# Four passes instead of six for the batch tails' second token product, a last MLP that ends block by block, and idle matmuls in other forms

## The chip, the cores and the metric

The kernel runs on one core of a Trainium2 chip, as one program. The metric is the device time of an execution in microseconds (us); runs of the same kernel are compared by their median. The engines are TensorE (PE in the rows; PEld is its weight load), VectorE (DVE), ScalarE (ACT), GpSimd (POOL) and SyncE (SP), which before the change issues every transfer of the kernel.

## The reference

Eight batches of 576 tokens go through sparse attention with 8 heads of 64 (heads 0 to 3 see the last 32 positions, heads 4 to 7 see positions of the same residue modulo 32), and then through a mixer in float32:

```
xt = x.transpose(0, 2, 1)
h = np.maximum(xt @ w_tok1, 0.0) @ w_tok2
u = x + h.transpose(0, 2, 1)
h2 = np.maximum(u @ w_ch1, 0.0) @ w_ch2
return (u + h2).astype(np.float32)
```

Here x is 576 tokens by 512 channels for each batch; w_tok1 is 576 x 256, w_tok2 256 x 576, w_ch1 512 x 1536 and w_ch2 1536 x 512.

## The kernel before

**Precision.** A float32 operand is kept as two fp32r tiles, a high part and the rest (`hh` and `hl`, `t2h` and `t2l`, `gh` and `gl`, `w2h` and `w2l`). A product is then three passes on TensorE: high by high, high by rest, rest by high. Weights arrive as 64-bit numbers; `convert` and `load_split` turn a piece of 128 x 512 into the two tiles with two steps on ScalarE, two on VectorE, one cast on ScalarE and one subtraction on GpSimd.

**Stages.** Tokens of a batch are cut into a main group of 512 (`MAIN`) and a tail of 64 (`TAIL`). The first token product (`tok1`, L489) and the second one for the main group (`tok2`, L515 and L520) work on one batch at a time, as does the channel MLP (`mlp`): twelve `up_proj` (L688: 12 matmuls into one bank, then `gh` on ScalarE at L691 and `gl` on VectorE at L692) and twelve `down_proj` (L703: 3 matmuls into each of the four accumulators `acc0` to `acc3`, one for each block of 128 channels). `down_proj(fc)` stands two steps behind `up_proj(fc)`. After the last `down_proj` VectorE adds the residual to each accumulator (L720) and SyncE writes the block out (L725, L729).

**Tails.** The 64 tail tokens of a batch are handled by `tok2_tail` (L524), which stands behind the first `up_proj` of the batch's MLP (behind the second `down_proj` step in batch 0). It makes 6 matmuls of 128x512 into one bank (L530); VectorE adds x in place (L532) and SyncE stores the 64 rows to a DRAM tile `u` (L533). In the eighth MLP `load_tails` (L538) reads the eight pieces back, `tail_u` (L543) transposes them, and a ninth MLP treats all 8 x 64 tail tokens as one group of 512. Its outputs are written by `out_tail` (L729), in rows of 64 tokens.

**Order.** TensorE, VectorE, ScalarE and GpSimd run in the order in which the code is written; the dictionary `after` puts pieces of other work behind given steps of an MLP. SyncE's order is chosen by a scheduler after the first stage. The strided heads of batches 2 to 7 are computed on GpSimd (products, L375) and VectorE (sums, L423 and L447) beside the MLPs.

**The start.** Before the first token product TensorE waits for x. `keep_busy(17)` (L640) fills that time with 17 matmuls on a zero bf16 tile `still` (L603). `still`, `idle_t` and these matmuls carry no result.

Of the kernel before, what the change touches and what calls it, by code (L numbers as in the profile page):

```python
# [10 lines left out]
F32 = mybir.dt.float32  # L11
F32R = mybir.dt.float32r
U32 = mybir.dt.uint32
# [3 lines left out]
ALU = mybir.AluOpType  # L17
# [3 lines left out]
B, H, S, D = 8, 8, 576, 64  # L21
HL = 4
ST = 32
DM = H * D
DT = 256
DF = 1536
P = 128
# [11 lines left out]
NCC = DM // P  # L39
NFC = DF // P  # L40
DV = D + 1
NSC = 5
# [9 lines left out]
MAIN = 512  # L52
TAIL = S - MAIN
# [3 lines left out]
def attn_mixer_kernel(ctx, tc, qkT, vw, qs, ks, vs, qksT, vsP, mask, mask2, w1, w2, wt1, wt2, outT):  # L57
    nc = tc.nc

    const = ctx.enter_context(tc.tile_pool(name="const", bufs=1))  # L60
# [17 lines left out]
    t1h = const.tile([P, NSC, DT], F32R, name="t1h")  # L78
    t1l = const.tile([P, NSC, DT], F32R, name="t1l")

    t2h = const.tile([P, 2, S + TAIL], F32R, name="t2h")
    t2l = const.tile([P, 2, S + TAIL], F32R, name="t2l")


    ud = [dram.tile([TAIL, DM], F32, name=f"u{b}") for b in range(B)]

    xd = [dram.tile([2 * S, DM], F32, name=f"x{p}") for p in range(B // 2)]

# [66 lines left out]

    def t2_tail(raws):

        src = (wt2[P * c:P * c + P, MAIN:].bitcast(U32).unsqueeze(1).to_broadcast([P, 2, 2 * TAIL]) for c in range(2))
        return load_split(raws, lambda: (t2h[:, :, MAIN:], t2l[:, :, MAIN:]), 4 * TAIL, *src)

    def w1_piece(raws, q, c):

# [361 lines left out]
    def tok2_tail(ps_t, x_t, h, b):  # L524

        pu = ps_t.tile([P, 512], F32, name="t")
        for m in range(2):
            hh, hl = h[m]
            for k, (l, r) in enumerate(((t2h, hh), (t2l, hh), (t2h, hl))):
                nc.tensor.matmul(pu, l[:, m, MAIN:], r, start=(m == 0 and k == 0), stop=(m == 1 and k == 2))  # L530
        rs = slice(64 * (b % 2), 64 * (b % 2) + 64)
        nc.vector.tensor_tensor(out=x_t[rs, NSC - 1], in0=pu[rs], in1=x_t[rs, NSC - 1], op=ALU.add)  # L532
        nc.sync.dma_start(out=ud[b], in_=x_t[rs, NSC - 1])  # L533

    def load_tails(u_t):

        for b in range(B):
            nc.sync.dma_start(out=u_t[64 * (b % 2):64 * (b % 2) + 64, b // 2], in_=ud[b])  # L538

    def tail_u(pool, ps_t, u_t, cc):  # L540
        pu = ps_t.tile([P, 512], F32, name="t")
# [40 lines left out]
    with tc.tile_pool(name="first", bufs=4) as first, \  # L582
         tc.tile_pool(name="raws", bufs=4, side="right") as raws, \
         tc.tile_pool(name="ps_a", bufs=6, space=PSUM) as ps_a, \
         tc.tile_pool(name="ps_m", bufs=2, space=PSUM) as ps_m:
        still = first.tile([P, 512], BF16, name="still", bufs=1)
        nc.vector.memset(still, 0.0)
        mask2_sb = first.tile([RP, RP], F32, name="mask2_sb", bufs=1)
        masks = first.tile([P, 5 * 64], BF16, name="masks", bufs=1)
        nc.sync.dma_start(out=mask2_sb, in_=mask2)  # L590
        loaded = [strided_load(first, 0, hp) for hp in range(2)]
        nc.sync.dma_start(out=mask_sb, in_=mask)
        nc.gpsimd.tensor_copy(
            out=mask2_b.rearrange("p (c k) -> p c k", k=RP), in_=mask2_sb.unsqueeze(1).to_broadcast([RP, 3, RP]))
        for c in range(5):
            nc.gpsimd.tensor_copy(out=masks[:, 64 * c:64 * c + 64], in_=mask_sb[:, FIRST.get(c, 0)])


        idle_t = ps_m.tile([P, 512], F32, name="t")

        def keep_busy(n):
            for _ in range(n):
                nc.tensor.matmul(idle_t, still[:, :P], still, start=True, stop=True)  # L603

        keep_busy(WARM)

# [12 lines left out]
        def steps(*gens):  # L619
            for g in gens:  # L620
                next(g, None)


        also = {0: [early[0], *units[:2], early[1], *units[2:], early[2], early[3]],
                4: [early[0]], 5: [early[0], early[4]], 6: [early[1]], 7: [early[1]], 8: [early[5]], 9: [early[2]], 10: [early[3], early[2]],
                11: [early[3]], 12: [early[4]], 13: [early[5], early[4]], 15: [early[5]]}
        for i in range(len(work) + 4):
            for k in (0, 2, 4):
                if 0 <= i - k < len(work):
                    if k == 2 and i >= BUSY:  # L630
                        keep_busy(2)
                    next(work[i - k], None)
            if i == 11:
                load_x(x_t, 0, slice(HL * D, DM))
                steps(early[6])
            steps(*also.get(i, ()))
        u = []
        mixes = [tok2(up0, ps_a, x_t, h, cc, u) for cc in range(NCC)]
        steps(early[7], mix)
        keep_busy(17)  # L640
        steps(mix, early[6], early[8], mix, early[6], mix, *mixes, mix, early[7], mix, *pieces[:4], early[7])
        steps(mixes[0], mixes[1], early[8], mixes[2], pieces[0], mixes[3], early[8])

# [18 lines left out]

    ps_t = Banks()

    def mlp(us, after, write):


        acc = [ps_acc.tile([P, MAIN], F32, name=f"acc{cc}") for cc in range(NCC)]
        g, res, count = {}, [], [0]

        def done():
            for f in after.get(count[0], ()):
                f()
            count[0] += 1

        def middle():
            for f in after.get(count[0] - 0.5, ()):
                f()

        def up_proj(fc, bank="h"):  # L680
            fs = slice(P * fc, P * fc + P)
            ph = ps_t.tile([P, MAIN], F32, name=bank)
            for cc in range(NCC):
                if cc == 2:
                    middle()
                uh, ul = us[cc]
                for k, (l, r) in enumerate(((w1h, uh), (w1l, uh), (w1h, ul))):
                    nc.tensor.matmul(ph, l[:, cc, fs], r, start=(cc == 0 and k == 0), stop=(cc == NCC - 1 and k == 2))  # L688
            gh = up.tile([P, MAIN], F32R, name="gh")
            gl = up.tile([P, MAIN], F32R, name="gl")  # L690
            nc.scalar.activation(out=gh, in_=ph, func=AF.Relu)  # L691
            nc.vector.scalar_tensor_tensor(out=gl, in0=ph, scalar=0.0, in1=gh.bitcast(F32), op0=ALU.max, op1=ALU.subtract)  # L692
            g[fc] = (gh, gl)
            done()

        def down_proj(fc):
            gh, gl = g.pop(fc)
            for cc in range(NCC):
                if cc == 2:
                    middle()  # L700
                cs = slice(P * cc, P * cc + P)
                for k, (l, r) in enumerate(((w2hl["h"], gh), (w2hl["h"], gl), (w2hl["l"], gh))):
                    nc.tensor.matmul(acc[cc], l[:, fc, cs], r, start=(fc == 0 and k == 0), stop=(fc == NFC - 1 and k == 2))  # L703
            if 4 <= fc < 4 + NCC:
                uh, ul = us[fc - 4]
                o_t = up.tile([P, MAIN], F32, name="ot", bufs=NCC)
                on_gpsimd(ALU.add, out=o_t, in0=uh.bitcast(F32), in1=ul.bitcast(F32))
                res.append(o_t)
            if fc < NFC - 1:
                done()  # L710

        up_proj(0)
        up_proj(1, "t")
        for fc in range(NFC):
            if fc + 2 < NFC:
                up_proj(fc + 2)
            down_proj(fc)

        for cc, o_t in enumerate(res):
            nc.vector.tensor_tensor(out=o_t, in0=acc[cc], in1=o_t, op=ALU.add)  # L720
            write(cc, o_t)
        done()

    def out_main(b):
        return lambda cc, o_t: nc.sync.dma_start(out=outT[P * cc:P * cc + P, S * b:S * b + MAIN], in_=o_t)  # L725

    def out_tail(cc, o_t):
        to = outT[P * cc:P * cc + P].rearrange("p (b s) -> p b s", s=S)
        nc.sync.dma_start(out=to[:, :, MAIN:], in_=o_t.rearrange("p (b t) -> p b t", t=TAIL))  # L729

    def strided_lane(pool, b, gs, got):
        for hp in range(HL // 2):
# [60 lines left out]
    for b in range(B):  # L793
# [52 lines left out]
        for i in range(24):  # L846
            if b or i >= 16:
                at(i, some_strided, 20 if b < 2 else 23)
        mlp(u, after, out_main(b))
        x_t, h, u = x_next["x"], x_next["h"], x_next["u"]  # L850
    mlp(u, {}, out_tail)


_OUT = (DM, B * S)
# [71 lines left out]
```

## Time and profile before

| what | value |
|---|---|
| median of 3 runs | 823.19 us (821.32 to 823.48) |
| profiled execution, first to last instruction | 821.2 us |
| TensorE busy | 799.8 us (97%) |
| VectorE, GpSimd, ScalarE busy | 449.8, 404.6, 229.6 us |
| mean granted TensorE clock | 0.996 |
| transfers | 80.80 MB, 98 GB/s on average |

The profile gives the span of the profiled execution, and no separate time for it; the three timed runs lie 0.1 to 2.3 us above that span. Matmuls overlap in the records: one of 128x512 is shown as 390 ns long, while the next one starts some 227 ns after it. So the distance between starts, not the duration, is the price of a matmul in a stream.

### The profile page before, as it was taken

The page shows a single profiled execution, that of the slowest core. Times are in us where ns is not written, and L with a number is a line of the kernel's source. Part 1 is how long each engine was busy: PE and PEld are TensorE (multiplying, and loading weights), DVE is VectorE, ACT ScalarE, POOL GpSimd, SP SyncE. Part 2 cuts the span into 40 slices and gives each one's busy share as a digit, 9 for nine tenths or more (in the row PEclk, how much of TensorE's full clock was granted, in tenths as well). Part 3 has the DMA queues.
Part 4 walks back from the last instruction along what each step waited for, and adds up shares of the span by engine and source line. Part 5 has one row for each costly group of instructions (what it writes and reads, how often), then busy time and mean ns, then how long its engine had stood idle before and what let it go on. Part 6 is the DMA issues. An engine that isn't in the chain of part 4 may idle for free.

```text
span 821.2 us, 14373 instructions
## 1 busy us (share of the span) xinstructions
PE 799.8 (97%) x5839; PEld 648.0 (79%) x5839; DVE 449.8 (55%) x990; ACT 229.6 (28%) x483; POOL 404.6 (49%) x305
## 2 busy tenths in 40 slices
PE   9899998999999999999999999999999999999996
PEld 6577776878788888887888888888888888888885
DVE  6866745777687576655856566667561213113112
ACT  5667755232121222212213021222121211102100
POOL 2223345959778694768767866686730102002000
PEclk9999999999999999999999999999999999999999
DMA  9586545233601440245113500551032003001002
GB/s 302 169 278 197 184 130 203 82 129 104 206 30 59 134 117 30 98 129 180 34 52 107 152 29 31 164 159 60 1 94 76 1 1 109 1 0 52 1 0 52
DMA packets 59166, 80.80 MB, mean 98 GB/s; under 512 B 22244, under 2 KB 37348, under 8 KB 59100
## 3 DMA queue, kind: packets, MB, share of 16 engines
q1 hardware_dynamic: 59100, 79.89, 31.0%
q8 instruction: 46, 0.75, 0.4%
q14 instruction: 20, 0.16, 0.1%
HBM read 60.41 MB, written 19.33 MB: 97 GB/s over the span
## 4 chain that ended last, share of the span: by engine, by line
PE 83%; DVE 4%; DMA 3%; ACT 3%; issue 1%; POOL 1%; SPq 1%; POOLq 0%; ACTq 0%; DVEq 0%
PE acc L703 33%; PE h L688 30%; PE t L520 5%; PE t L489 5%; PE t L688 3%; PE t L515 1%; PE t L530 1%; PE t L299 1%; DMA w_raw<-in_w 1%; PE t L271 1%; PE t L289 1%; DVE xhl L477 1%; ACT gh L691 1%; ACT w_rest L118 1%; DMA sa<-in_ks 1%
## 5 line engine op out<-in xcount | busy, mean ns | idle before, releaser
L375 POOL TENSOR_TENSOR sprod<-sa,ss 128x576 f32<-128x576 f32 (+8 forms) x108 | 153.2, 1450 | 78.2 <-issue 40.0
L375 POOL TENSOR_TENSOR sprod<-sa 128x576 f32<-128x576 f32 (+8 forms) x108 | 159.6, 1508 | 40.1 <-DVE ss L423 11.1
L692 DVE SCALAR_TENSOR_TENSOR gl<-h,gh 128x512 fp32r<-128x512 f32 x99 | 68.3, 690 | 200.6 <-ACT gh L691 200.6
L703 PE MATMUL acc<-gh,w2h 128*128 128x512 f32 x432 | 170.8, 395 | 0.0
L703 PE MATMUL acc<-gh,w2l 128*128 128x512 f32 x432 | 168.5, 390 | 0.0
L703 PE MATMUL acc<-gl,w2h 128*128 128x512 f32 x432 | 168.5, 390 | 0.0
L688 PE MATMUL h<-uh,w1h 128*128 128x512 f32 x396 | 158.0, 399 | 2.3 <-DVE gl L692 2.3
L688 PE MATMUL h<-ul,w1h 128*128 128x512 f32 x396 | 155.0, 391 | 0.0
L688 PE MATMUL h<-uh,w1l 128*128 128x512 f32 x396 | 154.6, 390 | 0.0
L691 ACT ACTIVATE gh<-h 128x512 fp32r<-128x512 f32 x99 | 59.0, 596 | 308.6 <-PE h L688 308.6
L375 POOL TENSOR_TENSOR ot<-uh,ul 128x512 f32<-128x512 f32 x36 | 49.7, 1388 | 139.7 <-DMA out_t<-ot 91.7
L703 PEld LDWEIGHTS acc<-gh,w2l 128*128 128x128 f32 x432 | 81.2, 188 | 17.3
L703 PEld LDWEIGHTS acc<-gh,w2h 128*128 128x128 f32 x432 | 81.3, 188 | 17.1
L703 PEld LDWEIGHTS acc<-gl,w2h 128*128 128x128 f32 x432 | 81.3, 188 | 16.3
L688 PEld LDWEIGHTS h<-uh,w1h 128*128 128x128 f32 x396 | 74.5, 188 | 19.4 <-DVE gl L692 3.1
L423 DVE TENSOR_REDUCE ss<-sprod 128x9 f32<-128x576 f32 (+8 forms) x108 | 80.1, 779 | 15.5 <-POOL sprod L375 15.2
L688 PEld LDWEIGHTS h<-ul,w1h 128*128 128x128 f32 x396 | 74.5, 188 | 16.1
L688 PEld LDWEIGHTS h<-uh,w1l 128*128 128x128 f32 x396 | 74.5, 188 | 14.6
L447 DVE TENSOR_REDUCE sa<-sprod 128x64 f32<-128x576 f32 (+8 forms) x108 | 79.5, 778 | 7.9 <-POOL sprod L375 7.7
L507 DVE TENSOR_TENSOR ul<-t,uh 128x512 fp32r<-128x512 f32 x36 | 24.8, 690 | 48.8 <-ACT uh L506 48.7
L489 PE MATMUL t<-xhl,t1h 128*128 128x512 f32 x144 | 45.2, 398 | 5.1 <-DVE xhl L474 2.4
L477 DVE TENSOR_TENSOR xhl<-x,xhl 128x512 fp32r<-128x512 f32 x32 | 37.5, 1191 | 12.9 <-ACT xhl L471 12.7
(122 smaller groups left out, 879.4 us busy)
## 6 DMA issues: line engine op xcount, KB each, us to landing
out_t<-ot SPq DMA_DIRECT2D x36, 256.0 KB
w_raw<-in_w SPq DMA_DIRECT2D x17, 512.0 KB
lqk<-in_qkT SPq DMA_DIRECT2D x20, 416.0 KB
lv<-in_vw SPq DMA_DIRECT2D x20, 390.0 KB
x<-x SPq DMA_DIRECT2D x28, 256.0 KB
xhl<-in_w SPq DMA_DIRECT2D x7, 512.0 KB
sa<-in_qs SPq DMA_DIRECT2D x6, 576.0 KB
sa<-in_ks SPq DMA_DIRECT2D x6, 576.0 KB
```

The costliest lines, as they stand in the source:

```text
L118: nc.scalar.activation(out=y_b[:, :, 0], in_=raw_b[:, :n, 3], func=AF.Identity, bias=below, scale=1.0 / 32)
L375: i = nc.gpsimd.tensor_tensor(op=op, **operands)
L423: nc.vector.tensor_reduce(out=s_t[:, i, :i + 1], in_=pr.rearrange("p (n d) -> p n d", d=D), axis=AX.X, op=ALU.add)
L447: nc.vector.tensor_reduce(out=o_t[:, i], in_=pr.rearrange("p (d n) -> p d n", n=i + 1), axis=AX.X, op=ALU.add)
L477: apart.append(nc.vector.tensor_tensor(out=xlo, in0=x, in1=xh.bitcast(F32), op=ALU.subtract))
L489: nc.tensor.matmul(ph[m], l[:, c, P * m:P * m + P], r, start=(c == 0 and k == 0), stop=(c == NSC - 1 and k == 1))
L507: nc.vector.tensor_tensor(out=ul, in0=pu, in1=uh.bitcast(F32), op=ALU.subtract)
L520: nc.tensor.matmul(pu, l[:, cs], r[:, m, :MAIN], start=False, stop=(m == 1 and k == 2), skip_group_check=True)
L688: nc.tensor.matmul(ph, l[:, cc, fs], r, start=(cc == 0 and k == 0), stop=(cc == NCC - 1 and k == 2))
L691: nc.scalar.activation(out=gh, in_=ph, func=AF.Relu)
L692: nc.vector.scalar_tensor_tensor(out=gl, in0=ph, scalar=0.0, in1=gh.bitcast(F32), op0=ALU.max, op1=ALU.subtract)
L703: nc.tensor.matmul(acc[cc], l[:, fc, cs], r, start=(fc == 0 and k == 0), stop=(fc == NFC - 1 and k == 2))
```

## The change

The edits, in the order of the diff:

- **Tail product.** `t2h` now holds, behind its 512 main columns, 64 columns of the high part and 64 of the rest of w_tok2's tail. One stationary operand of 128 columns therefore yields both products, in rows 0 to 63 and 64 to 127 of the bank. Two moving operands (`hh`, `hl`) and two chunks make 4 matmuls. VectorE adds x to the upper half; ScalarE copies the lower half to the other 64 rows of `x_t`; 128 rows are stored instead of 64. The piece `t2_tail` that is loaded and converted has 128 columns instead of 256.
- **Loading the tails.** 16 loads instead of 8, the second halves into two `xhl` tiles, and four additions of 128x512 on GpSimd.
- **Last MLP.** With `held=3` the last three `down_proj` are not done one after the other but block by block: nine matmuls for a channel block, then its addition and its write. The last block is added and written in two halves, the second of them issued by ScalarE.
- **Output layout.** The output keeps the main groups of all batches first and the tail group behind them, in rows of 512 tokens each; the host puts them in order.
- **Idle matmuls.** Instead of 17 on `still`: eight fp32r ones of 128x512 and four of 128x256 on parts of `t1h` and `t1l`, and then six on `still`.

```diff
-    t2h = const.tile([P, 2, S + TAIL], F32R, name="t2h")
-    t2l = const.tile([P, 2, S + TAIL], F32R, name="t2l")
+    t2h = const.tile([P, 2, MAIN + 2 * TAIL], F32R, name="t2h")
+    t2l = const.tile([P, 2, MAIN], F32R, name="t2l")
...
-    ud = [dram.tile([TAIL, DM], F32, name=f"u{b}") for b in range(B)]
+    ud = [dram.tile([2 * TAIL, DM], F32, name=f"u{b}") for b in range(B)]
...
-        src = (wt2[P * c:P * c + P, MAIN:].bitcast(U32).unsqueeze(1).to_broadcast([P, 2, 2 * TAIL]) for c in range(2))
-        return load_split(raws, lambda: (t2h[:, :, MAIN:], t2l[:, :, MAIN:]), 4 * TAIL, *src)
+        src = (wt2[P * c:P * c + P, MAIN:].bitcast(U32) for c in range(2))
+        return load_split(raws, lambda: (t2h[:, :, MAIN:MAIN + TAIL], t2h[:, :, MAIN + TAIL:]), 2 * TAIL, *src)
...
-            hh, hl = h[m]
-            for k, (l, r) in enumerate(((t2h, hh), (t2l, hh), (t2h, hl))):
-                nc.tensor.matmul(pu, l[:, m, MAIN:], r, start=(m == 0 and k == 0), stop=(m == 1 and k == 2))
-        rs = slice(64 * (b % 2), 64 * (b % 2) + 64)
-        nc.vector.tensor_tensor(out=x_t[rs, NSC - 1], in0=pu[rs], in1=x_t[rs, NSC - 1], op=ALU.add)
-        nc.sync.dma_start(out=ud[b], in_=x_t[rs, NSC - 1])
+            for k, r in enumerate(h[m]):
+                nc.tensor.matmul(pu, t2h[:, m, MAIN:], r, start=(m == 0 and k == 0), stop=(m == 1 and k == 1))
+        nc.vector.tensor_tensor(out=x_t[:TAIL, NSC - 1], in0=pu[:TAIL], in1=x_t[:TAIL, NSC - 1], op=ALU.add)
+        nc.scalar.copy(out=x_t[TAIL:, NSC - 1], in_=pu[TAIL:])
+        nc.sync.dma_start(out=ud[b], in_=x_t[:, NSC - 1])
...
-        for b in range(B):
-            nc.sync.dma_start(out=u_t[64 * (b % 2):64 * (b % 2) + 64, b // 2], in_=ud[b])
+        halves = [xp.tile([P, 2, DM], F32, name="xhl") for _ in range(2)]
+        for p in range(B // 2):
+            l_t = halves[p // 2][:, p % 2]
+            for b in (2 * p, 2 * p + 1):
+                rs = slice(TAIL * (b % 2), TAIL * (b % 2) + TAIL)
+                nc.sync.dma_start(out=u_t[rs, p], in_=ud[b][:TAIL])
+                nc.sync.dma_start(out=l_t[rs], in_=ud[b][TAIL:])
+            nc.gpsimd.tensor_tensor(out=u_t[:, p], in0=u_t[:, p], in1=l_t, op=ALU.add)
...
-        keep_busy(17)
+        rows = t1h[:, 0:2].rearrange("p c n -> p (c n)")
+        for n, (l, r, cols) in enumerate((
+                (t1h, rows, 0), (t1h, rows, 0), (t1h, rows, 0), (t1h, rows, 0), (t1l, rows, 1), (t1h, rows, 0), (t1l, rows, 1), (t1h, rows, 0),
+                (t1l, rows[:, :256], 0), (t1h, rows[:, :256], 1), (t1l, rows[:, :256], 0), (t1h, rows[:, :256], 1))):
+            nc.tensor.matmul(idle_t[:, :r.shape[1]], l[:, 2, P * cols:P * cols + P], r, start=True, stop=True)
+        for n in (0, 1, 2, 3, 0, 1):
+            nc.tensor.matmul(idle_t, still[:, P * n:P * n + P], still, start=True, stop=True)
...
+        def down_block(fc, cc):
+            gh, gl = g[fc]
+            cs = slice(P * cc, P * cc + P)
+            for k, (l, r) in enumerate(((w2hl["h"], gh), (w2hl["h"], gl), (w2hl["l"], gh))):
+                nc.tensor.matmul(acc[cc], l[:, fc, cs], r, start=(fc == 0 and k == 0), stop=(fc == NFC - 1 and k == 2))
...
-            down_proj(fc)
+            if fc < NFC - held:
+                down_proj(fc)
...
-            nc.vector.tensor_tensor(out=o_t, in0=acc[cc], in1=o_t, op=ALU.add)
-            write(cc, o_t)
+            for fc in range(NFC - held, NFC):
+                down_block(fc, cc)
+            parts = [slice(0, MAIN)] if not held or cc < NCC - 1 else [slice(0, MAIN // 2), slice(MAIN // 2, MAIN)]
+            for part in parts:
+                nc.vector.tensor_tensor(out=o_t[:, part], in0=acc[cc][:, part], in1=o_t[:, part], op=ALU.add)
+                write(cc, o_t, part)
...
+        def write(cc, o_t, part):
+            queue = nc.scalar if part.start else nc.sync
+            queue.dma_start(out=outT[P * cc:P * cc + P, MAIN * b + part.start:MAIN * b + part.stop], in_=o_t[:, part])
...
-    mlp(u, {}, out_tail)
+    mlp(u, {}, out_group(B), held=3)
```

The order of the instructions at three places follows; names are those of the code, with the number of the buffer behind them.

TensorE at the tail of batch 1, before: the last matmul of the first `up_proj`, the six of the tail, and the first of the second `up_proj`.

```order
L688 MATMUL h<-ul,w1h 128x512
L530 MATMUL t<-hh_1651,t2h 128x512
L530 MATMUL t<-hh_1651,t2l 128x512
L530 MATMUL t<-hl_1652,t2h 128x512
L530 MATMUL t<-hh_1653,t2h 128x512
L530 MATMUL t<-hh_1653,t2l 128x512
L530 MATMUL t<-hl_1654,t2h 128x512
L688 MATMUL t<-uh,w1h 128x512
```

The same place of the changed kernel:

```order
L699 MATMUL h<-ul,w1h 128x512
L529 MATMUL t<-hh_1651,t2h 128x512
L529 MATMUL t<-hl_1652,t2h 128x512
L529 MATMUL t<-hh_1653,t2h 128x512
L529 MATMUL t<-hl_1654,t2h 128x512
L699 MATMUL t<-uh,w1h 128x512
```

Two matmuls of 128x512 are gone, and nothing else stands differently there.

TensorE at its end, before: the last `down_proj`, whose four accumulators take turns.

```order
L703 MATMUL acc0_7424<-gh_7744,w2h_862 128x512
L703 MATMUL acc0_7424<-gl_7745,w2h_862 128x512
L703 MATMUL acc0_7424<-gh_7744,w2l_863 128x512
L703 MATMUL acc1_7425<-gh_7744,w2h_862 128x512
L703 MATMUL acc1_7425<-gl_7745,w2h_862 128x512
L703 MATMUL acc1_7425<-gh_7744,w2l_863 128x512
L703 MATMUL acc2_7426<-gh_7744,w2h_862 128x512
L703 MATMUL acc2_7426<-gl_7745,w2h_862 128x512
L703 MATMUL acc2_7426<-gh_7744,w2l_863 128x512
L703 MATMUL acc3_7427<-gh_7744,w2h_862 128x512
L703 MATMUL acc3_7427<-gl_7745,w2h_862 128x512
L703 MATMUL acc3_7427<-gh_7744,w2l_863 128x512
```

The end of the changed kernel: the last matmul of block 2 and the nine of block 3, whose `gh` and `gl` come from the last three `up_proj`.

```order
L711 MATMUL acc2_7433<-gh_7751,w2l_864 128x512
L711 MATMUL acc3_7434<-gh_7691,w2h_863 128x512
L711 MATMUL acc3_7434<-gl_7692,w2h_863 128x512
L711 MATMUL acc3_7434<-gh_7691,w2l_864 128x512
L711 MATMUL acc3_7434<-gh_7722,w2h_863 128x512
L711 MATMUL acc3_7434<-gl_7723,w2h_863 128x512
L711 MATMUL acc3_7434<-gh_7722,w2l_864 128x512
L711 MATMUL acc3_7434<-gh_7751,w2h_863 128x512
L711 MATMUL acc3_7434<-gl_7752,w2h_863 128x512
L711 MATMUL acc3_7434<-gh_7751,w2l_864 128x512
```

The 36 matmuls of the last three steps are the same in number. Each of the first three blocks is complete nine matmuls before the next one instead of three.

GpSimd at its end in the changed kernel; before, twelve additions at L375 stand there in a row.

```order
L375 TENSOR_TENSOR ot<-uh,ul 128x512 x4
L543 TENSOR_TENSOR x<-x,xhl 128x512 x4
L375 TENSOR_TENSOR ot<-uh,ul 128x512 x8
```

The four new additions stand ahead of the residual sums `ot` of the eighth and the ninth MLP.

## Rows read from the trace of the kernel before

**Rows 1.** The page: busy time by engine, and the chain by line.
```profile
PE 799.8 (97%) x5839; PEld 648.0 (79%) x5839; DVE 449.8 (55%) x990; ACT 229.6 (28%) x483; POOL 404.6 (49%) x305
...
PE acc L703 33%; PE h L688 30%; PE t L520 5%; PE t L489 5%; PE t L688 3%; PE t L515 1%; PE t L530 1%; PE t L299 1%; DMA w_raw<-in_w 1%; PE t L271 1%; PE t L289 1%; DVE xhl L477 1%; ACT gh L691 1%; ACT w_rest L118 1%; DMA sa<-in_ks 1%
```

**Rows 2.** TensorE's waits from 240 us to the end: total, times, longest (us).
```profile
PE h L688 <- DVE gl L692: 1.8, 1, 1.8
PE t L489 <- DVE xhl L477: 0.3, 1, 0.3
```

**Rows 3.** Timeline at the tail of batch 2: start and duration (us), instruction, idle before.
```profile
255.42 0.39 PE L530 MATMUL t<-hh,t2h 128*128 128x512 f32 x1
...
256.78 0.39 PE L688 MATMUL t<-uh,w1h 128*128 128x512 f32 x1
...
256.98 0.68 DVE L532 TENSOR_TENSOR x<-t,x 64x512 f32<-64x512 f32 x1
...
259.76 0.60 ACT L691 ACTIVATE gh<-t 128x512 fp32r<-128x512 f32 x1 [3.54 <-PE t L688]
```

**Rows 4.** The chain that ended last, at the tails of batches 0 and 1.
```profile
65.93 1.39 PE t L530 x6
...
165.79 1.36 PE t L530 x6
```

**Rows 5.** Timelines of ScalarE and VectorE behind the tail of batch 0.
```profile
67.03 0.87 ACT L118 ACTIVATE w_rest<-w_raw,small 128x512 uint8<-128x512 uint8 x1
...
67.77 0.67 DVE L532 TENSOR_TENSOR x<-t,x 64x512 f32<-64x512 f32 x1
...
73.60 0.52 ACT L342 ACTIVATE es<-es 126x378 f32<-126x378 f32 x1 [2.63 <-DVE es L341]
```

**Rows 6.** Timeline of GpSimd in the ninth MLP.
```profile
750.54 5.02 POOL L375 TENSOR_TENSOR ot<-uh,ul 128x512 f32<-128x512 f32 x4 [62.99 <-DMA out_t<-ot]
```

**Rows 7.** Timeline of the end.
```profile
807.36 0.69 DVE L692 SCALAR_TENSOR_TENSOR gl<-h,gh 128x512 fp32r<-128x512 f32 x1 [4.75 <-ACT gh L691]
...
812.91 2.73 DVE L720 TENSOR_TENSOR ot<-acc,ot 128x512 f32<-128x512 f32 x4 [4.85 <-PE acc L703]
...
813.63 3.35 SPq L729 DMA_DIRECT2D out_t<-ot  x4
...
814.47 0.39 PE L703 MATMUL acc<-gh,w2l 128*128 128x512 f32 x1
```

**Rows 8.** SyncE's waits from 680 us to the end.
```profile
SPq L921 <- DMA out_t<-ot: 3.2, 1, 3.2
```

**Rows 9.** Windows: busy us of each engine, granted clock, share and GB/s of transfers.
```profile
750.00:751.00 1.00, 1.00 (x6) 0.78 (x6) 0.81 (x2) 0.20 (x1) 0.46 (x1) 1.00 1.05 381
815.00:816.00 1.00, 0.00 (x0) 0.00 (x0) 0.64 (x1) 0.00 (x0) 0.00 (x0) 1.00 0.99 221
```

**Rows 10.** Timeline of SyncE: a tail of 64 rows stored, and the next issue.
```profile
685.84 0.47 SPq L533 DMA_DIRECT2D u<-x  x1
688.20 5.12 SPq L538 DMA_DIRECT2D x<-u  x8
```

**Rows 11.** A VectorE group that reads a bank, by form: busy us, mean ns.
```profile
L341 DVE TENSOR_TENSOR es<-t,em 126x252 f32<-126x252 f32 x8 | 3.4, 420 | 0.3
```

**Rows 12.** Timeline of the idle matmuls and what follows them.
```profile
34.17 3.61 PE L603 MATMUL t<-still 128*128 128x512 bf16 x16 [0.81 <-issue]
...
37.06 1.14 ACT L471 CAST xhl<-x 128x512 fp32r<-128x512 f32 x2
...
37.73 0.73 PE L489 MATMUL t<-xhl,t1h 128*128 128x512 f32 x2
```

**Rows 13.** Windows as in group 9, around TensorE's stretch at the lower clock.
```profile
104.77:108.18 3.41, 3.41 (x11) 2.66 (x10) 1.07 (x7) 2.28 (x7) 0.00 (x0) 0.50 0.34 112
...
108.20:818.10 709.90, 699.77 (x4821) 574.27 (x4819) 375.49 (x766) 158.81 (x341) 374.76 (x267) 1.00 0.26 80
38.00:60.00 22.00, 20.81 (x99) 15.67 (x99) 14.30 (x24) 13.67 (x26) 5.04 (x5) 1.00 0.78 258
```

More of the change, by code (lines that the diff above doesn't have):

```diff
@@ L663, in attn_mixer_kernel, with mlp @@
     ps_t = Banks()
-    def mlp(us, after, write):
+    def mlp(us, after, write, held=0):
         acc = [ps_acc.tile([P, MAIN], F32, name=f"acc{cc}") for cc in range(NCC)]
@@ L694, in up_proj @@
             done()
+        def down_block(fc, cc):
[3 more added lines that the diff above has]
+                nc.tensor.matmul(acc[cc], l[:, fc, cs], r, start=(fc == 0 and k == 0), stop=(fc == NFC - 1 and k == 2))
         def down_proj(fc):
-            gh, gl = g.pop(fc)
             for cc in range(NCC):
@@ L700, in down_proj @@
                     middle()
-                cs = slice(P * cc, P * cc + P)
-                for k, (l, r) in enumerate(((w2hl["h"], gh), (w2hl["h"], gl), (w2hl["l"], gh))):
-                    nc.tensor.matmul(acc[cc], l[:, fc, cs], r, start=(fc == 0 and k == 0), stop=(fc == NFC - 1 and k == 2))
+                down_block(fc, cc)
             if 4 <= fc < 4 + NCC:
@@ L716, in mlp, with out_group @@
                 up_proj(fc + 2)
-            down_proj(fc)
+            if fc < NFC - held:
+                down_proj(fc)
         for cc, o_t in enumerate(res):
-            nc.vector.tensor_tensor(out=o_t, in0=acc[cc], in1=o_t, op=ALU.add)
-            write(cc, o_t)
-        done()
[L724 to L729, printed above, removed]
+            for fc in range(NFC - held, NFC):
+                down_block(fc, cc)
+            parts = [slice(0, MAIN)] if not held or cc < NCC - 1 else [slice(0, MAIN // 2), slice(MAIN // 2, MAIN)]
+            for part in parts:
+                nc.vector.tensor_tensor(out=o_t[:, part], in0=acc[cc][:, part], in1=o_t[:, part], op=ALU.add)
+                write(cc, o_t, part)
+        done()
+    def out_group(b):
+        def write(cc, o_t, part):
+            queue = nc.scalar if part.start else nc.sync
+            queue.dma_start(out=outT[P * cc:P * cc + P, MAIN * b + part.start:MAIN * b + part.stop], in_=o_t[:, part])
+        return write
     def strided_lane(pool, b, gs, got):
@@ L848, in attn_mixer_kernel @@
                 at(i, some_strided, 20 if b < 2 else 23)
-        mlp(u, after, out_main(b))
+        mlp(u, after, out_group(b))
         x_t, h, u = x_next["x"], x_next["h"], x_next["u"]
-    mlp(u, {}, out_tail)
+    mlp(u, {}, out_group(B), held=3)
 _OUT = (DM, B * S)
@@ L924 @@
     got = r.results[0]["out_t"]
-    return np.ascontiguousarray(got.T).reshape(B, S, DM)
+    main, tail = got[:, :B * MAIN].reshape(DM, B, MAIN), got[:, B * MAIN:].reshape(DM, B, TAIL)
+    return np.ascontiguousarray(np.concatenate([main, tail], axis=2).transpose(1, 2, 0))
```

## The prediction

> **What bounds the kernel now.** I read the page first: TensorE is busy for 97% of the span, and the chain that ended last lies on its matmuls for most of its length, above all those of the MLPs [rows 1]. A busy TensorE is not yet one that never waits, so I read its waits next. From 240 us on there are only 2.1 us of them in 580 us [rows 2]: there a matmul less is its price less. Before 220 us TensorE does wait now and then, so I looked at whether the chain passes through the tails of batches 0 and 1; both stand in it [rows 4]. Last I read the end. The last matmul starts at 814.47 us and ends at 814.86, VectorE's fourth addition ends at 812.91 + 2.73 = 815.64, SyncE's last issue at 813.63 + 3.35 = 816.98 [rows 7]; then SyncE waits another 3.2 us, until about 820.2, for the output to land [rows 8]. So 5.4 us pass between the last matmul and the landing, and the closing steps take 1.0 us more, to 821.2.
>
> **Tail product.** The six matmuls of a tail take from 255.42 to 256.78, 1.36 us or 227 ns each [rows 3]. Two of six go in each of 8 batches: 16 x 0.227 = 3.63 us. The 128 columns of the stationary operand and the 512 of the moving one stay, so I price a remaining pass as one of before. Bounds: all of it comes through (3.63), or that of batches 0 and 1 is lost in the waits before 220 us (6 x 0.453 = 2.72). I take 3.6, since both tails are in the chain.
>
> What this adds: a ScalarE copy in each batch, which stands behind VectorE's addition of the same tile. Its price is at most that of a 128x512 step there, 0.60 us [rows 3]. In batch 2 the addition ends at 257.66, the copy would end by 258.3, and ScalarE's next step waits for TensorE until 259.76, or 259.3 after the change: about 1 us of cover. Batch 0 is tighter. The addition ends at 68.44, so the copy at about 69.0, and the conversion step that began at 67.03 is queued behind it; it comes 2 us later, but ScalarE idles for 2.63 us before 73.60 [rows 5]. I cost both at nothing; without the cover batch 0 would pay some 1 us. The stored rows double and the loads go from 8 to 16, at 0.64 us an issue (5.12 / 8) [rows 10]: 5 us more on SyncE, late in the eighth MLP, with nothing but outputs behind them. The four GpSimd additions cost 4 x 1.25 = 5 us [rows 6]. They wait for the loads, near 700 us, and hold up the sums `ot` of the eighth MLP, which are wanted near 748 us; GpSimd is idle for 63 us there. Nothing again. The smaller `t2_tail` piece takes a few tenths off ScalarE near 54 us, where TensorE is busy anyway (20.81 of 22 us) [rows 13]: nothing.
>
> **The end.** TensorE's last 36 matmuls are as many as before, so its end moves only by a wait that is new. The group begins 35 matmuls before 814.47, at 806.53. The last `gl` is ready at 807.36 + 0.69 = 808.05 [rows 7]; before, 24 matmuls covered it, now it is wanted by the eighth, at 806.53 + 7 x 0.227 = 808.12, and its weight load begins 0.23 us earlier. If that load waits too, 0.2 us are lost; if TensorE also restarts slowly, 0.4; if not, 0. I take 0.2.
>
> Behind the last matmul: three of four blocks have been written by then, since their accumulators are complete 2.0 us apart. Of the last block VectorE adds 256 columns first. The nearest row is 420 ns for 252 columns [rows 11]; with the 0.1 us that lay between the first block's last matmul (nine ahead of 814.47, so it ended at 812.82) and its addition at 812.91 [rows 7], that half is done at +0.5 us and the other at +0.9, and its issue starts at +0.95. A 128 KB store took 2.36 us from its issue to the instruction that waited for it [rows 10]. So the landing is at +3.3 us instead of +5.4: 2.1 us saved. The large cause is visible: 256-byte rows move at 221 GB/s, 2 KB rows at 381 [rows 9], and all four blocks (1 MB, 4.9 us) came at once. Bounds: 128 rows spread the half wider than 64 and land 0.3 us sooner, 2.4 saved; the trace has no transfer that ScalarE issues, and if its first takes 1 us more, 1.1 are saved. I take 2.1.
>
> **Idle matmuls.** Seventeen at 0.216 us are 3.67 us. The new block is 8 x 0.227 + 6 x 0.216 = 3.11 us, and four with 256 columns between half and all of 0.227: 3.6 to 4.0 us. The first real matmul starts at 37.73, right when ScalarE's first `xhl` is done (37.06 + half of 1.14) [rows 12]; a block up to 0.1 us longer costs nothing, the longest some 0.2. I take 0.
>
> **Sum.** -3.6 - 2.1 + 0.2 = -5.5 us: a span of 815.7 instead of 821.2. The timed runs lie up to 2.3 us above that span, so I take the difference from their median: 823.2 - 5.5 = 817.7. The terms' bounds give a gain between 2.72 + 1.1 - 0.4 - 0.2 = 3.2 and 3.6 + 2.4 + 0.1 = 6.1 us, that is 817.1 to 820.0 for this case.
>
> **Rivals.**
> 1. *The gain is eaten by work that TensorE does not pace.* VectorE and GpSimd's strided heads and the transfers that carry them set when x of a batch arrives; the 1.8 us wait [rows 2] hangs on such a chain. If GpSimd's pace decides there, the four tails ahead of it (4 x 0.453 = 1.8 us) are lost: 819.5. Against it: it is the one long wait after 240 us. Chance 0.14; in a third of that, more waits appear and the gain falls under 2.5 us.
> 2. *The end stays long*, since ScalarE's first transfer starts late. Then about 1.1 of 2.1 us: 818.7. Chance 0.08.
> 3. *The clock.* Between 104.77 and 108.18 us the granted clock is 0.50, the lower of the two levels (1.2 GHz), behind a stretch in which TensorE was busy only in part; 3.41 us at half speed cost 1.7 us of work [rows 13]. Shifted work can bring a second such stretch (819.4, chance 0.06) or take this one away (816.0, chance 0.06).
> 4. *The other side: the new idle matmuls don't hold the clock.* If TensorE enters the first token product at the lower level and stays there through most of 38 to 60 us, its 20.81 us of work there take up to that much longer; with half of it, +10 us: 828. It decides from 8 us on, five stretches like that of rival 3. Against it: fp32r matmuls of 128x512 held the full clock from 108.20 to 818.10 us [rows 13], and six of the old kind stay in front of the product. Chance 0.03.
> 5. *A pass left out frees less than a pass costs*, say only its weight load, on average 648.0 / 5839 = 0.111 us [rows 1]. Then the term is 1.8 us and the time 819.5. Chance 0.02: the starts lie 227 ns apart [rows 3], and the six are back to back.
>
> By that rule of the Trainium skill which speaks for rival 5 (TensorE: Matmul & The Clock Gate, section Back-to-back issue gap), a stream of weight loads and matmuls of 512 columns is sustained at about 131 ns each; as an estimate from that page the term would be 16 x 0.131 = 2.1 us and the time 819.2. The trace disagrees, with 227 ns for fp32r operands, and the trace decides.
>
> **How the numbers follow.** The forecast has 0.61. The rivals' times lie between 816.0 and 819.5, but for the fourth and the worse part of the first; a range from 815.0 to 820.6 leaves out no more than those and a clock that turns out better together with everything else. About 0.3% (2.5 us) is what a measurement of this kernel can tell from no change. Faster than 820.7: all but the worse part of rival 1 (0.05), pairs of rivals 1 to 3 together (0.04) and rival 4, so 0.87. Within 0.3%: 0.09. Slower: 0.04.
>
> **What the profile of the changed kernel would show.** The four tail matmuls should take 0.91 us from the first's start to the next `up_proj`, in all eight batches; TensorE's waits from 240 us on should stay near 2 us, and no new row should name ScalarE's copy, the GpSimd additions or a load of `xhl`. The last matmul should end 3.4 us earlier (about 811.4), with at most one wait of 0.2 us for the last `gl`; from there to the span's end 4.3 instead of 6.4 us. At 38 us the granted clock should be 1.00. I would be wrong if the last matmul ended less than 2.5 us earlier (rivals 1, 3 or 5; the waits and the clock's windows tell which), or if the span ran on for more than 5 us behind it (rival 2).

## The result, and the profile after

| | before | changed |
|---|---|---|
| median (lowest to highest), us | 822.26 (821.3 to 823.48), 4 runs | 815.68 (814.2 to 816.46), 4 runs |
| span of the profiled execution, us | 821.24 | 813.81 |
| last matmul ends, us | 814.86 | 810.04 |
| from there to the span's end, us | 6.38 | 3.77 |

The ratio is 0.9909, with a 95% interval of 0.988 to 0.9937: 6.6 us between the medians, 7.4 us between the two profiled spans. Of the 7.4 us, 4.8 lie ahead of the last matmul's end and 2.6 behind it. The forecast had 3.4 and 2.1.

The page of the changed kernel first (busy us, share, instructions; then the chain by line). It answers to [rows 1]: TensorE is busy for 4.0 us less, and the chain lies on its matmuls as before. (The lines of the chain here account for a smaller share of the span than before, so their shares don't compare one by one.)

```profile
PE 795.8 (98%) x5824; PEld 645.6 (79%) x5824; DVE 450.7 (55%) x991; ACT 234.4 (29%) x491; POOL 409.3 (50%) x309
...
PE acc L711 23%; PE h L699 21%; PE t L489 3%; PE t L520 3%; PE t L699 2%; PE t L515 1%; DMA x<-ls 1%; PE t L299 1%; PE t L271 1%; PE t L529 0%; PE t L289 0%; ACT ls L284 0%; PE t L548 0%; DVE gl L703 0%; ACT gh L702 0%; SPq L387 0%
```

Here is the tail itself, in the timeline of TensorE at batch 2 (start, duration), against [rows 3].

```profile
254.21 0.39 PE L529 MATMUL t<-hh,t2h 128*128 128x512 f32 x1
254.43 0.39 PE L529 MATMUL t<-hl,t2h 128*128 128x512 f32 x1
254.66 0.39 PE L529 MATMUL t<-hh,t2h 128*128 128x512 f32 x1
254.89 0.39 PE L529 MATMUL t<-hl,t2h 128*128 128x512 f32 x1
255.11 0.39 PE L699 MATMUL t<-uh,w1h 128*128 128x512 f32 x1
```

From the first tail matmul to the MLP's next one 0.90 us pass instead of 1.36. In the trace the eight tails take 0.906 to 0.915 us each.

TensorE's waits from 240 us to the end (total, times, longest), against [rows 2], and below them the one wait of its weight loads in the last 34 us:

```profile
PE h L699 <- DVE gl L703: 1.0, 1, 1.0
PE t L489 <- DVE xhl L477: 0.2, 1, 0.2
```

```profile
PEld acc L711 <- DVE gl L703: 0.2, 1, 0.2
```

The long wait, near 370 us, is 0.8 us shorter. No row names the copy on ScalarE, the new additions or the loads. The end, in the timeline (against [rows 7]) and in SyncE's waits (against [rows 8]):

```profile
809.65 0.39 PE L711 MATMUL acc<-gh,w2l 128*128 128x512 f32 x1
810.13 0.76 DVE L739 TENSOR_TENSOR ot<-acc,ot 128x256 f32<-128x256 f32 x2 [1.35 <-PE acc L711]
810.97 0.37 ACTq L747 DMA_DIRECT2D out_t<-ot  x1
```

```profile
SPq L941 <- DMA out_t<-ot: 1.8, 2, 1.4
```

VectorE's halves are done at 810.89, 0.85 us behind the last matmul; ScalarE issues at +0.93; the span ends at +3.77. By the trace the second half has landed at 812.7, that is 1.8 us behind its issue, and 1.1 us of closing steps follow.

The windows of the granted clock, against [rows 13] (busy us of each engine, clock, transfers):

```profile
103.77:107.19 3.42, 3.42 (x11) 2.70 (x10) 1.09 (x6) 2.30 (x7) 0.00 (x0) 0.50 0.33 105
107.20:813.70 706.50, 696.99 (x4806) 571.44 (x4805) 376.81 (x767) 162.99 (x348) 379.76 (x271) 1.00 0.26 83
```

While TensorE works there is one stretch at the lower level (1.2 GHz), as before and at the same place; the first token product, from 37.15 us, runs at 1.00. The mean clocks of the two spans differ all the same, 0.996 and 0.998: before, the last 3.1 us of the span, behind the last matmul, are at 0.50 as well, and in the changed kernel the last 0.1 us. That costs nothing, but it means that equal mean clocks of the two kernels don't stand for equal stretches.

So the parts that the trace of this pair shows are: tails 16 x 0.227 = 3.6 us; end 2.6 us; wait for the last `gl` -0.1 us (the last matmul gained 4.82 us, the last `gh` 4.92); the wait near 370 us 0.8 us; and 0.5 us in small shifts, of which 0.44 stand at the start of the first tail already. Of the 0.44, 0.13 stand at the first matmul of the first `up_proj`, and 0.31 come between it and the tail. Here are these two instructions before, changed, in idle_only (six passes) and in tails_only (four), two kernels of the experiments:

```profile
53.83 0.39 PE L688 MATMUL h<-uh,w1h 128*128 128x512 f32 x1
65.77 0.39 PE L530 MATMUL t<-hh,t2h 128*128 128x512 f32 x1
```

```profile
53.70 0.39 PE L699 MATMUL h<-uh,w1h 128*128 128x512 f32 x1
65.33 0.39 PE L529 MATMUL t<-hh,t2h 128*128 128x512 f32 x1
```

```profile
53.70 0.39 PE L694 MATMUL h<-uh,w1h 128*128 128x512 f32 x1
65.64 0.39 PE L530 MATMUL t<-hh,t2h 128*128 128x512 f32 x1
```

```profile
54.52 0.39 PE L693 MATMUL h<-uh,w1h 128*128 128x512 f32 x1
66.14 0.39 PE L529 MATMUL t<-hh,t2h 128*128 128x512 f32 x1
```

The distance is 11.94, 11.63, 11.94 and 11.62 us. Over all profiles it is 11.92 to 11.94 us in the five kernels with six passes and 11.61 to 11.63 us in the seven with four, so the 0.31 us are the change's own too. What the tail edit alters ahead of the first tail is the piece `t2_tail`, with 128 columns instead of 256; its first step on ScalarE, before and changed:

```profile
53.53 0.61 ACT L118 ACTIVATE w_rest<-w_raw,small 128x256 uint8<-128x256 uint8 x1
```

```profile
53.40 0.46 ACT L118 ACTIVATE w_rest<-w_raw,small 128x128 uint8<-128x128 uint8 x1
```

Its three steps there take 0.36 us less together (0.46 + 0.33 + 0.30 instead of 0.61 + 0.43 + 0.41). The time comes out at the 32 score matmuls (L187) ahead of the tail. The third of them starts 0.06 us behind the end of the second `gl` in both kernels (63.88 behind 63.82, 63.45 behind 63.39); that `gl` stands behind its `gh`, and `gh` on ScalarE behind the steps of the weight pieces.

What was left for the experiments is whose the wait near 370 us is. The 0.13 us differ between runs: the first `up_proj` starts anywhere from 53.06 to 54.90 us in the seven profiles without a low stretch ahead of it.

### The profile page after: what moved, and what is told of

It reads as the page before. It is cut to its first block, busy times and chain, and to the rows that moved or that the text cites. A ratio compares the mean times of both kernels' runs of the same rounds, so it can differ in the third digit from the quotient of the medians.

```text
span 813.8 us, 14384 instructions
## 1 busy us (share of the span) xinstructions
PE 795.8 (98%) x5824; PEld 645.6 (79%) x5824; DVE 450.7 (55%) x991; ACT 234.4 (29%) x491; POOL 409.3 (50%) x309
## 4 chain that ended last, share of the span: by engine, by line
PE 54%; DMA 1%; ACT 0%; DVE 0%; SPq 0%; DVEq 0%; issue 0%; ACTq 0%
PE acc L711 23%; PE h L699 21%; PE t L489 3%; PE t L520 3%; PE t L699 2%; PE t L515 1%; DMA x<-ls 1%; PE t L299 1%; PE t L271 1%; PE t L529 0%; PE t L289 0%; ACT ls L284 0%; PE t L548 0%; DVE gl L703 0%; ACT gh L702 0%; SPq L387 0%
## 5 line engine op out<-in xcount | busy, mean ns | idle before, releaser
L375 POOL TENSOR_TENSOR sprod<-sa,ss 128x576 f32<-128x576 f32 (+8 forms) x108 | 153.2, 1450 | 75.9 <-issue 39.4
L375 POOL TENSOR_TENSOR sprod<-sa 128x576 f32<-128x576 f32 (+8 forms) x108 | 159.6, 1505 | 39.3 <-DVE ss L423 11.1
L375 POOL TENSOR_TENSOR ot<-uh,ul 128x512 f32<-128x512 f32 x36 | 49.8, 1392 | 94.7 <-DVE xhl L477 47.4
```

The costliest lines, as they stand in the source:

```text
L375: i = nc.gpsimd.tensor_tensor(op=op, **operands)
```

## The experiments

The kernels take single parts of the change, one puts a wait elsewhere, and one is the changed kernel again. "Span" and "end" (from the last matmul's end to the span's end) are those of the profiled execution; the ratios are to the kernel before, measured beside it.

| kernel | median us (runs) | before beside it | ratio, 95% | span | end |
|---|---|---|---|---|---|
| tails_only | 818.53 (12) | 822.77 (29) | 0.9948 (0.9931 to 0.9966) | 817.4 | 6.38 |
| end_only | 821.09 (12) | 822.77 (29) | 0.9988 (0.997 to 1.0006) | 818.8 | 3.77 |
| idle_only | 822.16 (12) | 822.77 (29) | 0.9997 (0.9972 to 1.0023) | 821.5 | 6.37 |
| without_idle | 815.72 (6) | 822.77 (29) | 0.9919 (0.9895 to 0.9943) | 814.2 | 3.77 |
| changed_again | 815.70 (12) | 822.21 (17) | 0.9926 (0.9904 to 0.9948) | 820.0 | 3.77 |
| scores_later | 812.64 (6) | 822.21 (17) | 0.9899 (0.9863 to 0.9935) | 810.2 | 3.77 |
| layout_only | 821.27 (1) | 822.21 (17) | one run | 819.5 | 3.91 |
| order_only | 819.52 (1) | 822.21 (17) | one run | 817.7 | 4.67 |
| last_whole | 825.16 (1) | 821.72 (1) | one run | 823.4 | 3.85 |
| halves_one_queue | 818.24 (1) | 821.72 (1) | one run | 816.5 | 3.82 |

The last column repeats to 0.01 us wherever the code of the end is the same (before, tails_only, idle_only; changed, end_only, without_idle, changed_again, scores_later). The times don't: within most of these kernels the runs lie 5 us apart and more. An edit of the end can therefore be settled by one profile, and none of the small terms by a time.

**tails_only.** The kernel before with `t2h` and `t2l` as changed, `t2_tail`, `tok2_tail` and `load_tails`:

```diff
-            for k, (l, r) in enumerate(((t2h, hh), (t2l, hh), (t2h, hl))):
+            for k, r in enumerate(h[m]):
```

> The kernel before with one part of the change: four passes in the tails and the halves added on GpSimd; output layout, end and idle matmuls as before. Theory (each part gives what its own rows show, and the rest of the 7.4 us is a wait near 370 us that differs from run to run): 3.6 us faster at the same clock, with 0.4 to 0.5 us at each of the eight tails and no other lasting step. Rival 1 (fewer tail passes also shorten the wait near 370 us): 4.4 us, and that wait is 1.0 us here instead of 1.8. Rival 2 (the parts help each other only together): under 3 us.

Measured: 4.3 us faster (2.8 to 5.7), and eight tails of 0.906 to 0.915 us. The time alone can't tell the theory's 3.6 us from rival 1's 4.4. From 240 us to the end TensorE has one row of waits left, so the copies, the 16 loads and the additions cost nothing there:

```profile
PE h L693 <- DVE gl L697: 0.9, 1, 0.9
```

That is the wait near 370 us, about as short as rival 1 had it; whether the tails shorten it is decided by the next kernels.

**end_only, idle_only, without_idle.** The kernel before with the layout, `held=3` and the halves; the kernel before with the new idle matmuls; the changed kernel with

```diff
-        rows = t1h[:, 0:2].rearrange("p c n -> p (c n)")
...
+        keep_busy(17)
```

> The kernel before with one part of the change: the down projections of the last three blocks of hidden channels of the last MLP by channel block, and the grouped output layout with the last block in two halves on two queues. Theory: 2.5 us faster (2.6 from the last matmul to the span's end, less 0.1 for the last gl), and nothing anywhere ahead of 760 us. Rival (the 2 KB rows of the layout also relieve the transfers of the other MLPs): over 3 us, with shorter waits before 760 us.

> The kernel before with one part of the change: the idle matmuls ahead of the first token product in the new forms. Theory: no change (within 0.3 us at the same clock), the first token product starts when its xhl is ready, as before. Rival (the new block ends earlier or holds the clock better, and that is what the 0.4 to 0.6 us ahead of the first tail come from): 0.5 us faster, with the first gh of the first MLP that much earlier.

> The changed kernel with the 17 idle matmuls of before in place of the new ones; all else as changed. Theory: as fast as the changed kernel (within 0.3 us at the same clock), so the other two parts alone give the whole gain. Rival: 0.5 us slower than the changed kernel.

Measured: the idle forms do nothing that shows either way, alone (0.9997, that is from 2.3 us faster to 1.9 slower) or taken back (815.72 against 815.68 and 815.70). The traces agree within finer bounds: the first token product starts at 37.64 us in idle_only against 37.73 before, and the 0.31 us ahead of the first tail are not there (11.94 us, as before), so the rival falls. end_only has the 2.6 us in its profile (3.77 instead of 6.38), but its times are only 1.0 us better by the ratio (from 2.5 faster to 0.5 slower): the expected 2.5 us is the edge of that interval, so the profile, not the time, shows this gain. The rival of over 3 us falls by the time. And the wait near 370 us, in the profiles of end_only, idle_only, layout_only and order_only, which all have the six passes of before:

```profile
PE h L688 <- DVE gl L692: 0.7, 1, 0.7
```

```profile
PE h L694 <- DVE gl L698: 1.1, 1, 1.1
```

```profile
PE h L688 <- DVE gl L692: 1.0, 1, 1.0
```

```profile
PE h L688 <- DVE gl L692: 0.4, 1, 0.4
```

In all eleven profiles other than that of before it lies between 0.4 and 1.1 us, with four passes or with six; 1.8 us stood in that one only. So rival 1 falls: fewer passes don't shorten that wait. The 0.8 us then belong to that one execution of the kernel before, as far as its single profile can say.

**layout_only, order_only.** The end taken apart: the grouped output layout with the order of before, and the new order with rows of 256 B (both write whole blocks on SyncE). The lines show what differs from the end of the changed kernel:

```diff
-    mlp(u, {}, out_group(B), held=3)
+    mlp(u, {}, out_group(B))
```

```diff
+        to = outT[P * cc:P * cc + P].rearrange("p (b s) -> p b s", s=S)
+        nc.sync.dma_start(out=to[:, :, MAIN:], in_=o_t.rearrange("p (b t) -> p b t", t=TAIL))
...
+    mlp(u, {}, out_tail, held=3)
```

> The kernel before with the grouped output layout alone: the last MLP writes rows of 2 KB instead of 256 B, all else as before, its four blocks all complete at the end and go out on SyncE. Theory (the rows are the larger cause): VectorE's fourth addition ends 0.8 us behind the last matmul, the store lands 2.1 us later, 1.0 us close: 4.0 us from the last matmul to the end, against 6.4 before and 3.8 changed. Rival (1 MB at once is the larger cause, whatever the rows): 5 us or more.

> The kernel before with only the order of the down projections of the last MLP changed (last three blocks of hidden channels by channel block); rows of 256 B, whole blocks, all on SyncE as before. Theory (the rows are the larger cause): 4.9 us from the last matmul to the end: addition to 0.9 us, issue of 1.1 us, 1.9 us to the landing, 1.0 us closing. Rival (1 MB at once is the larger cause): 4.0 us or less.

Measured: 3.91 and 4.67 us. The layout alone brings 2.47 of the 2.61 us; the order alone 1.71; together hardly more than the layout. Behind the new order, where one block alone is left for the end, the rows are still worth 0.82 us (4.67 against the 3.85 of last_whole below). Timeline and SyncE's wait of layout_only, then of order_only:

```profile
813.65 2.73 DVE L728 TENSOR_TENSOR ot<-acc,ot 128x512 f32<-128x512 f32 x4 [4.86 <-PE acc L700]
...
814.37 2.37 SPq L736 DMA_DIRECT2D out_t<-ot  x4
...
815.20 0.39 PE L700 MATMUL acc<-gh,w2l 128*128 128x512 f32 x1
```

```profile
SPq L736 <- DVE ot L728: 63.9, 4, 63.1
SPq L930 <- DMA out_t<-ot: 1.7, 1, 1.7
```

```profile
812.70 0.39 PE L700 MATMUL acc<-gh,w2l 128*128 128x512 f32 x1
813.18 0.69 DVE L728 TENSOR_TENSOR ot<-acc,ot 128x512 f32<-128x512 f32 x1 [1.35 <-PE acc L700]
```

```profile
SPq L929 <- DMA out_t<-ot: 2.2, 1, 2.2
```

In layout_only VectorE adds the four blocks as late as before: its fourth addition ends at 816.38, 0.79 us behind the last matmul, and SyncE's last issue ends at 814.37 + 2.37 = 816.74, 0.36 us behind that addition. Before, it ended 1.34 us behind it [rows 7], and the wait behind the issue was 3.2 us [rows 8] where it is 1.7 here. The rows shorten both, though 1 MB still goes at once.

**last_whole, halves_one_queue.** The changed kernel without halves, and with both halves on SyncE:

```diff
-            parts = [slice(0, MAIN)] if not held or cc < NCC - 1 else [slice(0, MAIN // 2), slice(MAIN // 2, MAIN)]
+            parts = [slice(0, MAIN)]
```

```diff
-            queue = nc.scalar if part.start else nc.sync
+            queue = nc.sync
```

> The changed kernel with the last block of the last MLP added and written whole on SyncE, not in halves on two queues. Theory (with rows of 2 KB a store of 256 KB lands hardly later than one of 128 KB): 3.9 us from the last matmul to the end, as with the layout alone, 0.1 us more than changed. Rival (the smaller store is what lands sooner): 4.3 us or more.

> The changed kernel with both halves of the last block issued by SyncE. Theory (ScalarE's queue starts as fast as SyncE's, and SyncE is free when the second half is added): 3.8 us from the last matmul to the end, as changed. Rival (ScalarE's first transfer is late): 3.5 us or less, that is shorter than changed.

Measured: 3.85 and 3.82 us against 3.77. ScalarE's queue is not late and gains 0.05 us; the halves gain 0.08. The whole block of last_whole is issued at 820.35 us, 0.81 behind the last matmul, and lands 2.0 us later; the second half of the changed kernel is issued later, at +0.93, and lands 1.8 us behind that. So the smaller store lands some 0.25 us sooner, and half of that goes to its later issue. By the Trainium skill, DMA: Bandwidth & Descriptors, section Latency and other measured facts, a transfer carries a fixed cost of about 2 us, most of it the receipt from the target memory. The totals here, 1.8 and 2.0 us, agree in size; the share of the receipt does not show, since the trace of the changed kernel has the last packet at 812.4 us and the landing only 0.35 us behind it.

**changed_again.** The changed kernel unchanged.

> The changed kernel itself once more, for its spread and its clock beside the kernel before. Theory (6.1 us of the 7.4 us in the profiled pair are the change: 3.6 tails, 2.6 end, less 0.1; the rest is a wait near 370 us and a clock that differ from run to run): a median 6 to 7 us below that of before, with runs at a mean clock of 0.996 some 1.5 us above those at 0.998, and the wait near 370 us at about 1 us again. Rival (the wait near 370 us is shortened by the change): 7.4 us at the same clock.

Measured: 0.9926, that is 6.1 us (4.3 to 7.9), with medians 6.5 us apart; the wait near 370 us is 0.6 us. The runs spread from 813.36 to 822.82, and the spread goes with the clock: the five with a mean of 0.998 or more lie from 813.4 to 815.0 us, the four at 0.996 from 815.4 to 818.9, one at 0.992 at 819.1, the two at 0.985 at 821.8 and 822.8. The profiled execution is one of the last two (windows; the clock is the third number from the right):

```profile
4.85:8.27 3.42, 2.48 (x15) 1.60 (x13) 0.87 (x2) 0.00 (x0) 0.00 (x0) 1.00 1.02 290
8.27:28.75 20.48, 20.15 (x115) 16.96 (x116) 12.37 (x35) 10.17 (x22) 3.48 (x7) 0.50 0.84 273
```

From 8.27 us the clock is at 0.50 for 20.48 us, and the span is 6.2 us longer than in the pair's profile. Four of the 29 runs of the kernel before, with mean clocks from 0.980 to 0.984, lie at 827.7 to 833.0 us: such times come with or without the change, though no profile shows where the stretches of those four lay.

**scores_later.** The stretch near 104 us stands right behind a pause of TensorE, here in the changed kernel:

```profile
100.33 0.46 PE L222 MATMUL t<-lv,ls 64*32 64x65 f32 x32
102.12 0.27 PE L187 MATMUL t<-lqk 64*32 64x64 f32 x2 [1.34 <-issue]
102.84 0.45 PE L187 MATMUL t<-lqk 64*32 64x64 f32 x30 [0.45 <-DVE lx L237]
```

The score matmuls (L187) of one unit of local heads stand behind the value matmuls (L222) of another and need banks that VectorE has still to empty. The edit moves them behind six matmuls of the up projection and three small ones:

```diff
-            for g, steps in zip(rest, ((0, 1.5, 2.5, 3.5), (2, 4.5, 5.5, 6.5), (5, 7.5, 8.5, 9.5), (7, 9.5, 10.5, 11.5)), strict=True):
+            for g, steps in zip(rest, ((0, 1.5, 2.5, 3.5), (2, 4.5, 5.5, 6.5), (5, 7.5, 8.5, 9.5), (7, 10, 10.5, 11.5)), strict=True):
```

> The changed kernel with the score matmuls of one unit of local heads (the fourth unit of the first MLP) placed half an up projection and three small matmuls later, behind six matmuls of the MLP instead of ahead of them; otherwise the same. TensorE waits 1.3 and 0.45 us there near 102 us for banks that VectorE empties, and the granted clock is 0.50 for 3.4 us right after. Theory (the low stretch follows from that wait): the wait is below 0.5 us, the stretch at 104 us is gone, and the span is 3 us shorter than that of the changed kernel. Rival 1 (the low stretch has nothing to do with the wait): 1.5 us shorter, with a stretch of 3.4 us as before. Rival 2 (VectorE's delay comes back at the next wait): no change.

Measured: TensorE's timeline there, and the clock over the whole span:

```profile
99.68 0.46 PE L222 MATMUL t<-lv,ls 64*32 64x65 f32 x32
100.07 0.50 PE L699 MATMUL h<-uh,w1h 128*128 128x512 f32 x1
...
101.57 0.49 PE L346 MATMUL t<-ident,es 126*126 126x126 f32 x3
102.13 0.70 PE L187 MATMUL t<-lqk 64*32 64x64 f32 x32
102.76 0.50 PE L711 MATMUL acc<-gh,w2h 128*128 128x512 f32 x1
```

```profile
4.80:810.30 805.50, 790.00 (x5812) 643.29 (x5814) 450.32 (x990) 232.74 (x490) 407.39 (x298) 1.00 0.32 102
```

The pause is gone and so is the stretch: 810.2 instead of 813.8 us of span, and a median 3.1 us below that of the changed kernel. Rival 2 falls; rival 1 too for this profile. But that is one profile, and a mean clock of 1.000, which leaves no room for a stretch, comes with the pause too: in 3 of the 16 runs of the changed kernel (813.4 to 814.4 us), against 3 of the 6 here (811.5 to 813.2 us). And the pause doesn't bring the stretch each time. Of the eleven other profiles, which all have it, nine show the stretch behind it; tails_only and order_only (windows below, in that order) don't.

```profile
105.00:112.00 7.00, 7.00 (x71) 5.83 (x70) 3.71 (x8) 5.24 (x12) 2.54 (x2) 1.00 0.11 31
```

```profile
105.00:112.00 7.00, 6.55 (x65) 5.42 (x64) 3.07 (x15) 5.63 (x14) 2.33 (x3) 1.00 0.32 97
```

So where the stretch comes, it comes behind the pause, and something else that no run here shows decides whether it comes; that the pause causes it is likely by these numbers and not shown. Two of the six runs of scores_later lie at 819.0 and 819.7 us with a mean clock of 0.987, close to the 0.985 of the run of changed_again whose profile shows the long stretch. By its median and its lowest run (811.5 us) this version is the fastest of all.

## Why the prediction was off

The direction and the mechanism were right; the gain came out larger, by 1.1 us in the first comparison's medians and by 0.6 us in the ratio of the second, changed_again. The 6.6 us between the medians lie beyond 6.1 us, the upper end of the terms' bounds. Two terms failed: the end was sized too small, beyond its own bound, and the smaller piece was put at nothing. Step by step:

- **Tail passes** (3.6 us): right. 0.91 us a tail was forecast, 0.906 to 0.915 measured, in all eight batches, and the waits before 220 us took nothing of it that stands out from the spread. From the first `up_proj` to the tail of batch 2, in the profiles whose one low stretch between them lies near 104 to 111 us, 201.59 and 201.32 us pass with six passes (before, end_only) and 199.93 to 200.51 with four (changed, without_idle, changed_again, halves_one_queue); that is 1.2 us less in the mean, which is what two tails of 0.45 us and the 0.31 us ahead of them make. By the Trainium skill, TensorE: Matmul & The Clock Gate, section Back-to-back issue gap, 131 ns a matmul would have made it 2.1 us, as an estimate from that page; the 0.227 us of the trace held, so rival 5 is out.
- **Copy, additions, loads** (0): right. The new additions ran at 687.6 and 690.9 us and the sums `ot` directly behind them; the next use of GpSimd was 47 us later.
- **The smaller piece** (0): wrong. It gave 0.31 us ahead of the first tail, in every profile of a kernel with four passes. The working had the few tenths off ScalarE and dropped them, since TensorE was busy for 20.81 of 22 us from 38 to 60 us. They came out behind that window, near 63.5 us, where the score matmuls stand behind ScalarE's and VectorE's work and no row names a wait, since the row that merges those matmuls (63.51 us, 0.82 us long) stretches over it.
- **The last `gl`** (+0.2): 0.1 lost behind a load that waited 0.2 us. Right in kind.
- **The end** (-2.1, at most -2.4): this is the step that failed most: 2.61 us, the same in every profile with this code. The working took 2.36 us from a store's issue to the instruction that waited for it [rows 10] as the time of a store. The store at the end measured 1.8 us. Of the 0.6 us between them, 0.13 are the instruction's own start: by the trace that store landed 2.2 us behind its issue. The other 0.47 lie between two stores of 128 KB, one of 64 rows of 2 KB and one of 128 rows of 1 KB, a difference that the working had bounded with 0.3; no run parts the number of rows from their length. VectorE's halves (+0.85 for +0.9), the issue (+0.93 for +0.95) and the closing (1.1 for 1.0) were right. The working also weighed order, halves and queue as causes of their own. layout_only shows that the layout alone has nearly all of it, and that with the layout in place the other three, with the wait for `gl` that the order brings, are together worth less than 0.1 us.
- **Idle matmuls** (0): right, added alone and taken back.
- **The base.** The sum was subtracted from 823.19 us, a median of three runs; 29 and 17 more gave 822.77 and 822.21. That is 0.4 to 1.0 us of the absolute error. And the pair of profiles differs by 0.8 us near 370 us and 0.13 at the start, which the change did not cause.
- **The clock** (rival 3): one low stretch in each of the pair's profiles while TensorE works, so neither branch came true in it. As a rival it was put wrongly: it was taken for something that the shifted work would decide, once; the runs show it differ between executions of one kernel.

Of the forecast's marks: the last matmul ended 4.8 us earlier instead of 3.4, of which 0.8 is the wait near 370 us and 0.31 the smaller piece; the end took 3.8 us instead of 4.3. With the terms as measured, 3.63 + 0.31 + 2.61 - 0.1 = 6.45 us; the second comparison's 6.1 (4.3 to 7.9) holds it, and the medians differ by 6.6, 6.5 and, for without_idle, 7.05 us. What stays open: where the 0.1 to 0.6 us more between the medians come from. Low stretches differ from run to run and are enough to account for it, but the times give only a mean clock, which does not say where a stretch lay.

## What to carry to other kernels

Before a pass is reordered to hide an output, look at the rows that it writes: a layout with rows of 2 KB gave here what the order, the halves and a second queue were built for. A high busy share does not make a term of another engine nothing: follow that engine's order to the next instruction that the busy one needs from it. Take a transfer's time from its issue to its landing, and from a transfer of the same shape. And a difference of one wait between two single profiles belongs to the change only if it stands in a second pair.

## What the runs showed of the hardware

- At the end of the kernel an issue of a store of 256 KB occupied SyncE for 0.33 us with rows of 2 KB, and for 0.53 (the shortest in order_only) to 1.13 us (the last one before) with rows of 256 B. Elsewhere rows of 2 KB can take longer too: 1.46 us for one at 425 us in the changed kernel.
- A store of 128 KB landed 2.2 us behind its issue with 64 rows of 2 KB (before, at 685.84 us) and 1.8 us with 128 rows of 1 KB (changed, at 810.97); 256 KB with 128 rows of 2 KB took 2.0 us (last_whole, at 820.35).
- VectorE begins to read a bank 0.1 us after the modelled end of the last matmul into it, in all orders of the end.
- The granted clock of one kernel differs between executions: at the start a stretch of 20.48 us at 0.50 in 2 of the 12 profiles, and from 103 to 112 us one of 3.41 us in 9. At half the clock the short one costs, as an estimate, half its length, 1.7 us; the long one came with a span 6.2 us longer.
